# Attention and two feed-forward layers on one core: score limits built on GpSimd after the opening, and four numbers of the planner changed

## The chip, the cores and the metric

One core of one Trainium2 chip runs the whole program. The metric is device time in microseconds (us), the median of three runs. The program is one launch: weights, queries, keys and values come from HBM, and the result goes back there.

## What is computed

Attention on 4 batches, 8 heads, 576 positions, head size 64, with two kinds of mask, followed by two gated feed-forward layers (2304 tokens, 512 -> 2048 -> 512):

```python
scores = scale * np.matmul(q, k.transpose(0, 1, 3, 2))
mask_local = (rel >= 0) & (rel < stride)                       # heads 0-3, stride 32
mask_strided = (rel >= 0) & (pos[None, :] % stride == pos[:, None] % stride)  # heads 4-7
scores = np.where(masks[None, :, :, :], scores, -1000000000.0)
attn = softmax(scores)                                          # written out in the reference
x = np.matmul(attn, v)                                          # -> (2304, 512)
h = x @ w_in;  g = h * (1.0 / (1.0 + np.exp(-1.702 * h)));  x = g @ w_out      # first layer
h = x @ w_in;  g = h * (1.0 / (1.0 + np.exp(-h)));          out = g @ w_out    # second layer
```

## The kernel before

The tokens are cut into eight chunks of 288 (half a sequence each). For every chunk there is an attention (four pairs of heads, one local and one strided head in each) and a first layer of 16 blocks `f` into the hidden size and 16 out of it. Attention of chunk c runs between the matrix products of chunk c-1's first layer. Chunk 0 works in float32 (L858 and L888); the later chunks work in pairs of float16 numbers, high and low part (L861 and L892). The second layer (L1173, L1284) follows when the last first layer is done, and works with factors of sums and differences of weight blocks.

A pair of heads goes through these steps: score products on TensorE (L707), masking and maxima on VectorE, subtraction of the maximum on GpSimd or VectorE (L731), exponential on ScalarE (L733), sum and inverse on VectorE (L736 to L741), scaling on GpSimd (L743), three transposes on TensorE (L749), a copy out of PSUM (L753 or L754), and the product with the values (L784). Chunk 0 adds its mask by products with `rep` and `mk` (L679, L682). The later chunks take the minimum with a tile of limits `mt`: eight small operations (L595, L596) on 32 partitions build it, two products with `rep` (L603) spread it to 128 partitions, and VectorE copies it back (L609).

Weights of the first layer are converted from 64-bit to 32-bit numbers on the core. A block is loaded (L301), ScalarE takes out two parts (L454, L306), ScalarE or VectorE takes the sign (L313, L311), VectorE joins bits (L317), GpSimd adds (L322), and ScalarE or VectorE sums squares for a scale (L473, L475). The blocks of the input weights are numbered f0 to f15 here, those of the output weights likewise. The weights of the second layer are converted beside chunks 1 to 6, parked in HBM (L523), loaded again in pairs (L546, L547), turned into factors by adds (L536) and splits into high and low parts (L412, L560), and stored (L563).

The order of the work on each engine is made when the program is built, by the class `Planner`: a list scheduler in which every task has engines with costs, a priority (a due time), the earliest time `at` from which it may be taken, and a `margin` between the end of what it needs and the moment when it is offered to its engine. A DMA's result is taken to be there 2 us plus `late` after the link has carried it. These numbers only decide the order: on the chip each engine runs its list in order, and waits on semaphores for what it needs. The numbers that the change touches are `ACT_AT`, the `at` of ScalarE's first step on each block of the input weights; `MARGIN[0]`, the margin ahead of the transposes of chunks 1 to 7; `MASK`, the priority of the limits; and the loads of factors, which have no `late`.

Of the kernel before, what the change touches and what calls it, by code (L numbers as in the profile page):

```python
# [37 lines left out]
WIN0, WINS = 18.0, 1.95  # L38
WOUT0, WOUTS = 49.0, 1.95
SCALE = (52.0, 84.0)  # L40
ACT_AT = 13.0
LATE = 5.0
WSI = T1 - 24.0
WSO = T1 + 4.0
# [1 line left out]
FACT = (270.0, 21.0)  # L46
ATT0 = {"load": (0.0, 5.5), "s": 5.0, "step": 1.5, "av": (20.6, 21.0)}
VSP, AHEAD, PLOW = 7.0, 8.0, 30.0
MARGIN = (0.4, 1.5, 0.6)
GORDER = (((0, 1), (0, 1, 2)), ((0, 1), (3,)), ((2, 3), (0, 1, 2, 3)))  # L50
SIGN, NSD, V2, MASK = 0.6, 4, 15.0, 30.0
NORM = (20.0, 24.0)
# [156 lines left out]
def attention_moe_moe2_kernel(  # L209
# [16 lines left out]
    nc = tc.nc  # L226
# [18 lines left out]
    w2s = nc.dram_tensor("w2_scratch", (2, KF, 128, 512), F32, kind="Internal").ap()  # L245
# [84 lines left out]
    at = actx.enter_context(tc.tile_pool(name="at", bufs=1))  # L330
# [56 lines left out]
    for i in range(4):  # L387
# [3 lines left out]
    P = Planner({"ps": range(8), "rq": [0], "rk": [0], "rv0": [0], "rv1": [0],  # L391
                 "ek": range(2), "eq": [1], "-": [], "pair": [1], "x1": [0], "sl": range(NSM), "pt": range(NPT), "t": range(NTS),
                 "cv": range(NCV), "f": range(NF)} | {f"g{f}": [0] for f in range(KF)}, 0.30)
# [121 lines left out]
    k_parked = {}  # L515
# [23 lines left out]
    fed = [None]  # L539

    def factors(i, prio, k_s):

        a, b, u, v = (P.buf("f") for _ in range(4))
        A, B, U, V = (lambda x=x: wm[:, x.idx] for x in (a, b, u, v))
        load, prio = prio, prio + PLOW
        ka = P.dma(load - 8, 0.25, lambda on: nc.sync.dma_start(out=A(), in_=w2s[0, i]), [k_s, k_parked[0, i], fed[0]], [a, b], at=load - 12)  # L546
        kb = P.dma(load - 8, 0.25, lambda on: nc.sync.dma_start(out=B(), in_=w2s[0, i + 8]), [ka, k_parked[0, i + 8]], (), [b])  # L547
        lo = lambda X: lambda: X()[:, 0:256]
        hi = lambda X: lambda: X()[:, 256:512]
        k1 = any_add(prio, lo(U), lo(B), hi(B), ALU.add, [kb], [u, v], [b])  # L550
        k3 = any_add(prio, lo(V), lo(A), lo(B), ALU.subtract, [ka, kb, k1], (), [v, a, b])
        k2 = any_add(prio, hi(U), lo(U), lo(A), ALU.subtract, [k1, ka], (), [u, a])
        k4 = any_add(prio, hi(V), hi(A), hi(U), ALU.subtract, [k2, k3], (), [v, a, u])
        parts = ((a, A, 0, 2, [ka]), (b, hi(B), 2, 1, [kb]), (u, U, 3, 2, [k1, k2]), (v, V, 5, 2, [k3, k4]))
        fed[0] = k1
        for x, src, m, w, deps in parts:
            o = P.buf("f")
            O = lambda o=o, w=w: wm[:, o.idx].bitcast(F16).rearrange("p (h e) -> p h e", h=2)[:, :, 0:256 * w]
            h = P.add(any_hi(256 * w), prio, lambda on, O=O, src=src: put(on, O()[:, 0], src(), sc["wi"][0]), [k_s, *deps], [o], [x])
            k = P.add(dve_t(256 * w), prio, lambda on, O=O, src=src: nc.vector.scalar_tensor_tensor(  # L560
                out=O()[:, 1], in0=src(), scalar=sc["wi"][0], in1=O()[:, 0], op0=ALU.mult, op1=ALU.subtract),
                [h], (), [x, o], two=True)
            P.dma(load + 2, 0.125 * w, lambda on, O=O, m=m, w=w: nc.sync.dma_start(  # L563
                out=wfs[i, :, :, m:m + w, :].rearrange("p h m e -> p h (m e)"), in_=O()), [k], (), [o])
# [24 lines left out]
    def mask_tile():  # L589

        def limits(on):
            e = nc.gpsimd if on == "POOL" else nc.vector
            for z, g, m in ((0, 0, 0), (0, 1, 1), (1, 0, 0), (1, 1, 2)):
                to = mt[0:32, z, :, g]
                e.tensor_scalar(out=to, in0=mk[0:32, m], scalar1=-1.0, scalar2=BIG, op0=ALU.is_ge, op1=ALU.mult)  # L595
                e.tensor_tensor(out=to, in0=to, in1=mk[0:32, m], op=ALU.add)  # L596
        kl = P.add({"POOL": 4.0, "DVE": 2.6}, MASK, limits)
        ks, kc = [], []
        for z in range(2):
            p = P.buf("ps")  # L600

            def mm(on, z=z, p=p):
                nc.tensor.matmul(banks[p.idx][:, 0:2 * W * NLB], lhsT=rep[0:32], rhs=mt[0:32, z].rearrange("p b g w -> p (b g w)"),  # L603
                                 start=True, stop=True)
            ks.append(P.add({"PE": 0.25}, MASK + 2.0, mm, [kl], [p]))
            kc.append((z, p))
        for z, p in kc:
            def copy(on, z=z, p=p):
                nc.vector.tensor_copy(out=mt[:, z].rearrange("p b g w -> p (b g w)"), in_=banks[p.idx][:, 0:2 * W * NLB])  # L609
                if z == 0:  # L610
                    nc.vector.memset(mt[0:32, 0, 0, 0, 0:32], NEG)
            k_mask.append(P.add({"DVE": 0.7}, MASK + 4.0, copy, ks, (), [p]))

    def attention(c, b):
# [46 lines left out]
        if c == 1:  # L661
            mask_tile()
# [255 lines left out]
    for i in range(KF // 2):  # L918
# [34 lines left out]
          for i in range(2)]  # L953
# [7 lines left out]
    P = Planner({"t": range(NS - 10), "f": range(NS - 10, NS - 6), "x": range(NS - 6, NS - 2), "xv": range(NS - 2, NS), "y": [], "w": [],  # L961
                 "ps": range(8), "r": range(NS + 2, NS + 6), "v": [NS, NS + 1, NS + 6, NS + 7]}, 0.29)
# [442 lines left out]
```

## Time and profile before

| | us |
|---|---|
| median of 3 runs (820.1 to 823.79) | 820.96 |
| profiled execution, device time | 820.78 |
| its span, first to last instruction | 819.0 |
| TensorE busy | 797.8 |
| VectorE busy | 607.0 |
| ScalarE busy | 500.7 |
| GpSimd busy | 376.3 |

The profiled execution takes 1.78 us more than its span, and 0.18 us less than the median. TensorE (PE in the rows) is busy in 97% of the span, so the 21.2 us in which it stands idle are what a change of order can gain, and new idle time is what it can lose. A row of a timeline reads: start, duration, engine, line, operation, what is written and read, and in square brackets how long the engine stood idle before it and what ended that.

### The profile page before, as it was taken

Reading aid. Unit: us, or ns where it says so; the run is one execution under the profiler, and the core shown is the slowest. Engines: PE = TensorE matmul, PEld = TensorE weight load, DVE = VectorE, ACT = ScalarE, POOL = GpSimd, SP = SyncE. Lnnn points to the kernel's source line nnn. Section 1 sums busy time; section 2 is a strip of 40 time slices with the busy share of each in tenths; the row PEclk is TensorE's granted clock in tenths of the full one; section 3 lists DMA queues with packets and bytes.
Section 4 is the critical chain, followed back from the end, with each engine's and each line's share of the span. In section 5 each row is a group of like instructions: output and inputs, shape, how many; then the busy total and the mean of one; then the engine's idle time right before and its main releaser. Section 6 shows DMA issues by size and latency. Waiting matters only on the chain.

```text
span 819.0 us, 22334 instructions
## 1 busy us (share of the span) xinstructions
PE 797.8 (97%) x8910; PEld 666.7 (81%) x8910; DVE 607.0 (74%) x1177; ACT 500.7 (61%) x930; POOL 376.3 (46%) x403
## 2 busy tenths in 40 slices
PE   5999999999999989999999999999999999999998
PEld 3776767878878768778787788888889988888887
DVE  8999889268479587697663727789987799878652
ACT  3898867398587685777843334645544766645510
POOL 4667654024126166275332525788977553221200
PEclk9999999999999999999999999999999999999999
DMA  9989600763827867545315725666767898656501
GB/s 271 407 216 277 146 22 10 190 195 107 233 100 225 270 220 243 178 149 173 123 61 199 279 81 168 227 223 212 221 211 259 287 318 274 231 192 224 177 28 52
DMA packets 91221, 157.26 MB, mean 192 GB/s; under 512 B 9380, under 2 KB 49644, under 8 KB 91116
## 3 DMA queue, kind: packets, MB, share of 16 engines
q1 hardware_dynamic: 90556, 154.45, 58.9%
q8 instruction: 70, 1.15, 0.6%
q10 hardware_dynamic: 560, 1.38, 0.6%
q14 instruction: 35, 0.29, 0.1%
HBM read 102.31 MB, written 53.48 MB: 190 GB/s over the span
## 4 chain that ended last, share of the span: by engine, by line
PE 74%; DVE 10%; DMA 6%; ACT 3%; POOL 3%; issue 2%; SPq 1%; DVEq 0%; POOLq 0%; ACTq 0%
PE aps L1173 10%; PE aps L1284 9%; PE aps L892 6%; PE aps L861 6%; PE hps L1173 5%; PE gps L1173 5%; PE hps L1284 4%; PE hps L892 4%; PE gps L1284 4%; PE gps L861 3%; PE hps L861 3%; PE aps L858 2%; PE gps L892 2%; DMA rv<-in_v_dram 2%; DMA rk<-in_k_dram 2%
## 5 line engine op out<-in xcount | busy, mean ns | idle before, releaser
L1173 PEld LDWEIGHTS <-wf 128*128 128x128 f16 x1680 | 150.6, 98 | 15.4
L1284 PEld LDWEIGHTS <-wf 128*128 128x128 f16 x1512 | 147.6, 98 | 17.5 <-DVE wf L996 0.4
L861 PEld LDWEIGHTS <-regA 128*128 128x128 f16 x1152 | 111.3, 98 | 29.6 <-issue 1.1
L892 PEld LDWEIGHTS <-regB 128*128 128x128 f16 x1152 | 111.7, 98 | 27.3
L989 POOL TENSOR_TENSOR tt<-tt 128x256 f32<-128x256 f32 (+2 forms) x87 | 83.2, 966 | 59.5 <-DVE wf L996 32.9
L322 POOL TENSOR_TENSOR wm<-wm 128x512 int32<-128x512 int32 x32 | 46.1, 1444 | 79.2 <-DVE wm L317 65.0
L861 PE MATMUL aps<-x,regA 128*128 128x288 f16 x612 | 81.2, 286 | 0.1
L984 ACT ACTIVATE wf<-tt,xsg 128x512 f16<-128x512 f32 x88 | 58.9, 712 | 27.9 <-DMA tt<-g_scratch 9.1
L996 DVE SCALAR_TENSOR_TENSOR wf<-tt,xsg,wf 128x512 f16<-128x512 f32 x88 | 72.4, 857 | 1.1 <-ACT wf L984 1.1
L892 PE MATMUL aps<-g,regB 128*128 128x288 f16 x480 | 62.6, 286 | 0.0
L1284 PE MATMUL aps<-regA,wf 128*128 128x256 f16 x480 | 58.1, 273 | 0.1
L1173 PE MATMUL aps<-xfa,wf 128*128 128x256 f16 (+1 forms) x528 | 53.1, 256 | 0.0
L892 PE MATMUL hps<-g,regB 128*128 128x288 f16 x384 | 50.8, 286 | 0.0
L743 POOL TENSOR_TENSOR prt<-prt,sus 128x384 f32<-128x384 f32 x32 | 31.5, 987 | 31.3 <-DVE sus L741 29.2
L1185 ACT ACTIVATE tt<-tt 128x512 f32<-128x512 f32 x39 | 24.4, 626 | 29.7 <-DVE tt L1180 29.5
L731 POOL TENSOR_TENSOR prt<-prt,nms 128x384 f32<-128x384 f32 x21 | 18.9, 898 | 49.6 <-DVE nms L729 43.3
L861 PE MATMUL gps<-x,regA 128*128 128x288 f16 x300 | 40.6, 286 | 0.7 <-DVE g L417 0.7
L417 DVE SCALAR_TENSOR_TENSOR g<-aps,sg,g 128x288 f16<-128x288 f32 x51 | 25.8, 512 | 19.6 <-ACT g L410 19.3
L1173 PE MATMUL aps<-g,wf 128*128 128x256 f16 x324 | 38.8, 273 | 0.0
L1284 PE MATMUL aps<-regB,wf 128*128 128x256 f16 x312 | 38.0, 273 | 0.0
L892 PE MATMUL gps<-g,regB 128*128 128x288 f16 x288 | 37.6, 286 | 0.0
L869 ACT ACTIVATE aps<-aps,invh 128x288 f32<-128x288 f32 x51 | 24.1, 478 | 16.4 <-PE aps L861 15.7
(317 smaller groups left out, 1813.7 us busy)
## 6 DMA issues: line engine op xcount, KB each, us to landing
tt<-g_scratch SPq DMA_DIRECT2D x76, 256.0 KB
g_scratch<-tt SPq DMA_DIRECT2D x64, 256.0 KB
w<-in_moe_w_out_dram SPq DMA_DIRECT2D x25, 512.0 KB
regB<-in_moe_w_in_dram SPq DMA_DIRECT2D x16, 512.0 KB
w<-in_moe_w_in_dram SPq DMA_DIRECT2D x16, 512.0 KB
w_scratch<-wm SPq DMA_DIRECT2D x32, 256.0 KB
regB<-g_scratch SPq DMA_DIRECT2D x32, 256.0 KB
wf<-in_factors SPq DMA_DIRECT2D x8, 896.0 KB
```

The lines of the kernel that those rows point to most:

```text
L322: nc.gpsimd.tensor_tensor(out=di, in0=m.bitcast(I32), in1=di, op=ALU.add)
L417: dve_t(n), prio, lambda on: nc.vector.scalar_tensor_tensor(out=lo(), in0=src(), scalar=s(), in1=hi(), op0=ALU.mult, op1=ALU.subtract),
L743: kno = P.add({"POOL": 1.0}, t + 8, lambda on: nc.gpsimd.tensor_tensor(out=sets(N), in0=sets(N), in1=wide(sus[:, sl.idx], 2 * NLB), op=ALU ...
L861: nc.tensor.matmul(o, lhsT=pvA[:, f, x, kk, :], rhs=x1[:, y, kk, :], start=(i == 0), stop=(i == 3 * KD - 1))
L869: a = P.add(act_t(HS), t + 2, lambda on, p=p: nc.scalar.activation(out=banks[p.idx][:, 0:HS], in_=banks[p.idx][:, 0:HS], func=AF.Gelu_appr ...
L892: nc.tensor.matmul(o, lhsT=pvB[:, f, u, dt * 128:(dt + 1) * 128], rhs=g1[:, w, f, :], start=(f == 0 and j == 0), stop=(f == KF - 1 and j = ...
L984: nc.scalar.activation(out=out, in_=in_, func=AF.Copy, scale=s)
L989: return P.add({e: x for e, x in any_add(n).items() if e in by}, prio, lambda on: (nc.gpsimd if on == "POOL" else nc.vector).tensor_tensor ...
L996: dve_t(n), prio, lambda on: nc.vector.scalar_tensor_tensor(out=lo(), in0=src(), scalar=s(), in1=hi(), op0=ALU.mult, op1=ALU.subtract),
L1173: nc.tensor.matmul(place(b, f), lhsT=wf[:, nf * g + f, x, wa, 128 * kk:128 * kk + 128], rhs=rhs.rearrange("p (h t) -> p h t", h=2) if n2 = ...
L1185: return P.add(act_t(512), t + 5, lambda on: nc.scalar.activation(out=sl(b), in_=sl(b), func=AF.Silu), after, (), [b], tab="silu")
L1284: nc.tensor.matmul(bank(b)[:, 256 * half:256 * half + 256], lhsT=fb[:, x, a, 128 * f:128 * f + 128], rhs=wt[:, 4 * p + f, z, wi, :], start ...
```

## The change

Five edits. The limits may only be built on GpSimd (before: GpSimd or VectorE), and not before the planner's time 30, and the two products that spread them not before 34. ScalarE's first step on the input weights may be taken from 17 on (before: 13). The margin ahead of the transposes of chunks 1 to 7 is 1.2 (before: 0.4). A load for factors is taken to be there 2 us later.

```diff
-ACT_AT = 13.0
+ACT_AT = 17.0
-MARGIN = (0.4, 1.5, 0.6)
+MARGIN = (1.2, 1.5, 0.6)
+FLATE = 2.0
-        ka = P.dma(load - 8, 0.25, lambda on: nc.sync.dma_start(out=A(), in_=w2s[0, i]), [k_s, k_parked[0, i], fed[0]], [a, b], at=load - 12)
-        kb = P.dma(load - 8, 0.25, lambda on: nc.sync.dma_start(out=B(), in_=w2s[0, i + 8]), [ka, k_parked[0, i + 8]], (), [b])
+        ka = P.dma(load - 8, 0.25, lambda on: nc.sync.dma_start(out=A(), in_=w2s[0, i]), [k_s, k_parked[0, i], fed[0]], [a, b], at=load - 12, late=FLATE)
+        kb = P.dma(load - 8, 0.25, lambda on: nc.sync.dma_start(out=B(), in_=w2s[0, i + 8]), [ka, k_parked[0, i + 8]], (), [b], late=FLATE)
-            e = nc.gpsimd if on == "POOL" else nc.vector
+            e = nc.gpsimd
-        kl = P.add({"POOL": 4.0, "DVE": 2.6}, MASK, limits)
+        kl = P.add({"POOL": 4.0}, MASK, limits, at=MASK)
-            ks.append(P.add({"PE": 0.25}, MASK + 2.0, mm, [kl], [p]))
+            ks.append(P.add({"PE": 0.25}, MASK + 2.0, mm, [kl], [p], at=MASK + 4.0))
```

What the change does to the lists of the engines stands at three places. Lines after the change are one higher than before (L604 is L603 of before).

TensorE's first rows, before the change: `mt` are the limits, `rep` spreads them, `mk` is the mask of chunk 0.

```order
L603 LDWEIGHTS rep
L603 MATMUL hps<-mt,rep 128x384
L603 LDWEIGHTS rep
L603 MATMUL hps<-mt,rep 128x384
L679 LDWEIGHTS rep
L679 MATMUL gps<-mk,rep 128x192
```

The same place after the change, and then the place to which the two products have gone, among chunk 0's products with the input weights (`x_75` is the attention's result):

```order
L680 LDWEIGHTS rep
L680 MATMUL hps<-mk,rep 128x192
...
L859 MATMUL aps<-x_75,regA 128x288 x16
L604 LDWEIGHTS rep
L604 MATMUL hps<-mt,rep 128x384
...
L859 MATMUL gps<-x_75,regA 128x288 x4
```

Chunk 0's scores now stand first on TensorE, and the spreading stands after six blocks of chunk 0's first layer. VectorE loses the eight operations that stood ahead of its first maxima; its two copies of `mt` move behind eleven of the bit joins (L317).

GpSimd's rows behind the setup of the masks, before: `prt` are attention's probabilities (scaled by L743), `regA` the converted input weights.

```order
L743 TENSOR_TENSOR prt<-prt,sus 128x384 x2
L322 TENSOR_TENSOR regA<-wm,regA 128x512
L743 TENSOR_TENSOR prt<-prt,sus 128x384 x2
L322 TENSOR_TENSOR regA<-wm,regA 128x512 x15
L322 TENSOR_TENSOR regB<-wm,regB 128x512 x7
```

The same place after:

```order
L744 TENSOR_TENSOR prt<-prt,sus 128x384 x4
L323 TENSOR_TENSOR regA<-wm,regA 128x512 x7
L596 TENSOR_SCALAR mt<-mk 32x3x64
L597 TENSOR_TENSOR mt<-mt,mk 32x3x64
...
L323 TENSOR_TENSOR regA<-wm,regA 128x512 x9
L323 TENSOR_TENSOR regB<-wm,regB 128x512 x6
```

All four pairs of chunk 0 are scaled ahead of the first weight block, and the eight operations of the limits stand between the blocks f6 and f7. On ScalarE the first weight block moves from behind the second exponential to behind the fourth exponential and the second copy of transposed probabilities.

GpSimd at the attention of chunk 5, where the first factors are made, before: `wm` holds factors, with `s` their scale; L536 is an add of a factor, L412 the high part of a split, L731 and L743 belong to pairs of heads.

```order
L731 TENSOR_TENSOR prt<-prt,nms 128x384
L322 TENSOR_TENSOR wm<-wm 128x512
L412 TENSOR_SCALAR wm<-wm,s 128x256
L536 TENSOR_TENSOR wm<-wm 128x256
L731 TENSOR_TENSOR prt<-prt,nms 128x384
L743 TENSOR_TENSOR prt<-prt,sus 128x384
L536 TENSOR_TENSOR wm<-wm 128x256
L412 TENSOR_SCALAR wm<-wm,s 128x512 x3
L743 TENSOR_TENSOR prt<-prt,sus 128x384
```

The same place after:

```order
L732 TENSOR_TENSOR prt<-prt,nms 128x384
L323 TENSOR_TENSOR wm<-wm 128x512
L744 TENSOR_TENSOR prt<-prt,sus 128x384
L732 TENSOR_TENSOR prt<-prt,nms 128x384
L413 TENSOR_SCALAR wm<-wm,s 128x256
L537 TENSOR_TENSOR wm<-wm 128x256 x3
L413 TENSOR_SCALAR wm<-wm,s 128x512
L744 TENSOR_TENSOR prt<-prt,sus 128x384
L413 TENSOR_SCALAR wm<-wm,s 128x512 x2
```

Ahead of chunk 5's second scaling there stood three splits in a row; now there stand three adds and one split, and the other splits follow it. On SyncE the second load of the first factors (L547 before, L548 after) stood behind a store of a parked block (L523) and now stands ahead of it. On TensorE, of the 24 transposes of chunks 2 to 7, 21 keep the same products between them and their scores; two have one block of products more (third pair of chunk 2, second of chunk 3) and one has one block less (second of chunk 6). In chunk 1 three of the four stand two to five products of L888 later against their scores. The list of the second layer is the same on all engines.

## Rows read from the trace of the kernel before

**Rows 1.** Busy time by stretch: length, engines, granted clock (PEclk), DMA share, GB/s.
```profile
0.00:20.00 20.00, 10.03 (x255) 6.94 (x256) 16.37 (x48) 7.71 (x15) 8.66 (x26) 1.00 0.90 267
...
60.00:107.00 47.00, 44.34 (x533) 32.46 (x533) 41.92 (x82) 35.47 (x72) 32.52 (x29) 1.00 0.75 188
107.00:140.00 33.00, 31.32 (x420) 24.71 (x420) 30.18 (x73) 25.75 (x52) 13.83 (x18) 1.00 0.06 19
...
290.00:310.00 20.00, 17.45 (x280) 13.67 (x278) 17.37 (x43) 16.99 (x30) 13.26 (x17) 1.00 0.67 215
```

**Rows 2.** Waits of TensorE: line, releaser, us in total, times, longest.
```profile
PE hps L603 <- DVE mt L596: 7.8, 2, 7.4
PE gps L749 <- POOL prt L743: 2.5, 4, 1.0
PE aps L431 <- DVE wtout L437: 1.1, 1, 1.1
```

**Rows 3.** Timeline of the opening, VectorE's row first, then TensorE's.
```profile
6.25 0.18 DVE L371 COPY rep<-idb 32x128 bf16<-32x128 bf16 x1
```
```profile
8.25 0.47 PE L603 MATMUL hps<-mt,rep 32*128 32x384 bf16 x1 [0.41 <-DVE mt L596]
8.66 0.50 PE L679 MATMUL gps<-mk,rep 128*128 128x192 bf16 x2
...
16.64 0.90 PE L749 MATMUL aps<-idt,prt 128*128 128x128 f32 x3 [0.85 <-POOL prt L743]
...
18.23 2.86 PE L784 MATMUL aps<-ptt,rv 64*64 64x32 f32 x82 [0.34 <-ACT ptt L753]
...
25.91 4.21 PE L858 MATMUL aps<-x,regA 128*128 128x288 f32 x8
```

**Rows 4.** SyncE's DMA queue from 0 to 16 us: packets, MB, share.
```profile
q1 hardware_dynamic: 891, 2.44, 55.3%
```

**Rows 5.** Timelines of ScalarE and GpSimd: a copy of probabilities; weight blocks f5 to f7 and f15.
```profile
17.70 0.47 ACT L753 ACTIVATE ptt<-aps 128x384 f32<-128x384 f32 x1
```
```profile
29.00 4.17 POOL L322 TENSOR_TENSOR regA<-wm,regA 128x512 int32<-128x512 int32 x3 [0.58 <-DVE wm L317]
...
51.16 1.28 POOL L322 TENSOR_TENSOR regA<-wm,regA 128x512 int32<-128x512 int32 x1 [1.30 <-DVE wm L317]
```

**Rows 6.** GpSimd's groups nearest to the limits: busy, mean ns, idle before.
```profile
L366 POOL TENSOR_SCALAR_AFFINE_SELECT mk<-mk 32x192 bf16<-32x192 bf16 x2 | 0.7, 346 | 0.0
```
```profile
L536 POOL TENSOR_TENSOR wm<-wm 128x256 f32<-128x256 f32 x22 | 18.1, 833 | 5.3 <-DVE wm L536 3.6 <-ACT ts L835 0.7 <-DMA wm<-w_scratch 0.5
```

**Rows 7.** VectorE's squares of L475 from 20 to 60 us: ns, least/median/most.
```profile
L475 DVE SCALAR_TENSOR_TENSOR jv<-regA x12: 680/1298/1741, 23.7 to 57.3; 128x512 uint8<-128x512 f32 x12
```

**Rows 8.** Timelines at the weights' scales; last, TensorE's later product with values.
```profile
59.93 0.28 PE L431 MATMUL aps<-wtin,ones 128*128 128x1 f32 x2
...
106.38 0.38 PE L431 MATMUL aps<-wtout,ones 128*128 128x1 f32 x2 [1.07 <-DVE wtout L437]
```
```profile
59.61 0.17 DVE L437 TENSOR_REDUCE wtin<-acc 128x1 f32<-128x16 f32 x1
```
```profile
102.75 1.27 POOL L322 TENSOR_TENSOR regB<-wm,regB 128x512 int32<-128x512 int32 x1
```
```profile
89.24 1.48 PE L784 MATMUL aps<-ptt,rv 64*64 64x32 f32 x80
```

**Rows 9.** Chunk 5's second pair: VectorE, GpSimd, TensorE, and SyncE's load of factors.
```profile
299.90 0.19 DVE L741 RECIPROCAL sus<-sus 128x6 f32<-128x6 f32 x1
```
```profile
300.11 0.97 POOL L412 TENSOR_SCALAR wm<-wm,s 128x512 f16<-128x512 f32 x1 [0.92 <-DMA wm<-w_scratch]
301.06 1.25 POOL L743 TENSOR_TENSOR prt<-prt,sus 128x384 f32<-128x384 f32 x1
```
```profile
302.36 0.55 PE L749 MATMUL hps<-idt,prt 128*128 128x128 f32 x3 [2.17 <-POOL prt L743]
```
```profile
288.11 0.39 SPq L547 DMA_DIRECT2D wm<-w_scratch  x1
```

## The prediction

> **What bounds the kernel now.** I read the busy time by stretch first [rows 1]. TensorE is idle 9.97 us in the first 20 us, 2.66 us from 60 to 107, 1.68 us from 107 to 140 and 2.55 us from 290 to 310: 16.9 of its 21.2 idle us. Everywhere else it runs without a gap, and the change takes no product away and adds none. So the time can only move through these stretches, and through new idle time. Then the waits of TensorE [rows 2]: 7.8 us are its first two products, which spread the limits and wait for VectorE to build them; next come transposes that wait for GpSimd's scaling, and the scale of the output weights (L431), which waits for VectorE's sum. Last the timelines around these waits [rows 3, 8, 9].
>
> From 20 to 107 us the other engines are nearly as full as TensorE: from 60 to 107 VectorE works 41.9 of 47 us [rows 1]. A microsecond that TensorE gains in the opening is kept only where conversion, squares and splits of the weights come earlier too.
>
> **The opening.** Before, chunk 0's first product (L679, 8.66) stands behind the two products with the limits [rows 3]. Its own needs are older: the copy into `rep` ends at 6.25 + 0.18 = 6.43, and the queries and keys of the first heads were issued at once. With the limits gone from VectorE and the spreading gone from the front of TensorE, it can start at about 6.5: 2.16 us earlier. Maxima, exponentials and scaling follow it in a chain that has no weight work in it now. The second transposes, 16.64 before, end at 16.64 + 0.90 - 2.16 = 15.38; ScalarE copies at once, because the weight step that stood between is behind it now (0.47 us, rows 5): 15.85. Before, the product with the values ran from 18.23 [rows 3]. Its other need is the values: behind queries, keys and two weight blocks SyncE's queue has to bring 608 + 1024 + 576 KB = 2.26 MB by the shapes of the transfers, and it had moved 2.44 MB by 16.0 us [rows 4]. That lets the product start between 15.9 and 16.3; I take 16.1, a shift of 2.1 us. Then 2.86 us of product, two sets of transposes (2 x 0.90), a copy (0.5): second product at 21.2, chunk 0's layer at about 23.9 instead of 25.91. Shift: **2.0 us**.
>
> What is late next? Weights f0 and f1. ScalarE starts them at 15.85 and needs four steps of about 0.6 us, VectorE a join, GpSimd 1.27 to 1.4 us for each [rows 5]: both are there by 20.9, 3 us ahead of 23.9, so this delay by `ACT_AT` costs nothing. Its cover is the attention; without it, the same weight steps would hold TensorE by up to what they are late.
>
> The limits now take GpSimd's time between f6 and f7. No row has this operation on GpSimd. From below, eight times 0.35 us (a select on the same 32 x 192 tile) is 2.8 us; from above, eight times 0.83 us (an add on 128 x 256) is 6.7 us [rows 6]. I take 3.3, near the first, whose tile it is. Block f7 was done at 33.17 [rows 5] and would be done at about 36.5, at worst 39.9. Sixteen blocks take (59.93 - 25.91) / 16 = 2.13 us each [rows 3, 8], so TensorE wants f7 at 23.9 + 7 x 2.13 = 38.8. Covered at the value that I take; at the upper bound TensorE loses 1.1 us. The last block, done at 52.4, is wanted at 55.8, and GpSimd waited for VectorE before each block there, so the delay shrinks on the way.
>
> The two spreading products now stand in the full stretch. They took 0.47 us each at the opening's pace; the product with the values shows that pace to be half of the later one (82 products in 2.86 us against 80 in 1.48 [rows 3, 8], with the granted clock column at 1.00 in both stretches [rows 1]). So they cost 2 x 0.23 = 0.46 us. If the pace should rise at the same moment as before and not 2 us earlier, another 1.0 us is lost. Net shift at 60 us: 2.0 - 0.46 = **1.5 us**, between 0.5 and 2.2.
>
> **From 60 to 140 us.** Here the shift meets two gates. The scale of the input weights (L431) ran at 59.93, hardly after VectorE's sum at 59.61; the scale of the output weights at 106.38, after a wait of 1.07 us, for a chain that starts from the last output block on GpSimd at 102.75 [rows 8]. Where those stay, TensorE arrives 1.5 us earlier and waits 1.5 us longer. Three things move them earlier: attention frees VectorE and ScalarE about 2 us sooner, VectorE has the limits less ahead of everything (1.8 us, from 6.43 to 8.25 [rows 3]), and ScalarE waited for products of chunk 0 that come sooner now. Three hold them: VectorE has the two copies of the limits among the weight steps now, squares that it did early are put off, and GpSimd does more subtractions (24 instead of 21). I let two thirds pass: **-1.0 us**. Bounds: nothing passes (0), or all of it and half of the idle 4.3 us of these two stretches with it (-3.7).
>
> **Transposes and factors.** The margin bites less than its name: 21 of 24 transposes of chunks 2 to 7 keep their distance from the scores, and the pair of the 2.17 us wait [rows 9] is one of them. What changes for it is GpSimd's list. Its inverse was ready at 300.09, but GpSimd was in a split (300.11 to 301.06), after 0.92 us of waiting for a load of factors, and the scaling took until 302.31. Now adds and one split stand ahead of this scaling, and the load of the second half, issued at 288.11 behind a store [rows 9], comes earlier in SyncE's list. Without the split the scaling would end at 300.09 + 0.1 + 0.85 = 301.0, so the wait shrinks from 2.17 to about 0.85: **-1.3 us**. Bounds: the whole 2.55 us of that stretch, or as much again lost at another pair whose scaling is now behind adds. The loads' `late` costs nothing by itself: the factors are read by the second layer alone, whose first products stand behind the whole last first layer.
>
> **The sum.** 820.78 - 1.0 - 1.3 = 818.5 for an execution like the profiled one; the median of before is 0.18 higher, so 818.7.
>
> **The rivals.** (a) *The parts add up.* The gates move with the opening and the waits of the first layers shrink: -3.7, and the 2.55 us of 290 to 310 go: 820.96 - 6.2 = 814.8. For it: VectorE's list is shorter by nine squares over the first part (they went to ScalarE, which had 11.5 us idle from 60 to 107). Against: the lists of TensorE around both gates are unchanged. Chance 0.32.
>
> (b) *The gates eat it.* VectorE gets back as interference what it gave away: squares of 512 columns took 680 ns alone and up to 1741 ns beside GpSimd's adds [rows 7], and now 3.3 us more GpSimd work lies in that stretch. Three or four squares slowed by about 0.6 us each are 2 us of VectorE, and both sums at the gates come no earlier. Then 1.5 us at the opening become 1.5 us more of waiting, the waits at 302 reappear at a neighbouring pair, and the time is 820.96. Chance 0.20. The Trainium skill's page "SBUF — State Buffer" (section "SBUF: two separate sides") states such a rule against this change: the port pair that VectorE and GpSimd share is held by one instruction for its whole length, and a VectorE operation with two inputs in SBUF waits until GpSimd's is done. The spread from 680 to 1741 ns agrees with it; by it alone this rival would be the forecast.
>
> (c) *Slower.* GpSimd's list becomes the gate of attention in chunks 5 to 7. Scaling now stands behind up to four adds of factors, which wait for loads; if in each of these three chunks one pair more waits as the second pair of chunk 5 did, 3 x 2.17 = 6.5 us are added, and the opening's gain is lost at the gates: 827.5. It decides from the point at which a load lands after GpSimd has reached its add and a scaling is ready behind it. For it: GpSimd waited for loads of factors already, 0.92 us ahead of this split [rows 9]. Against: the larger `late` places users later. Chance 0.10.
>
> **How the numbers follow.** Forecast 818.7 with chance 0.38; (a) 0.32, (b) 0.20, (c) 0.10. A measurement of this kernel tells 0.5%, 4.1 us, from no change, so faster means below 816.9 and slower above 825.1. Faster: (a), less its upper edge, plus the forecast's lower edge: 0.35. Slower: (c) nearly whole: 0.09. The same: 0.56. Range: below, (a) with the other half of the first layers' waits gone too (814.8 - 2.1 = 812.7); above, (b) with one new wait of 2.2 us, 823.2; what is beyond is (c) and little of (a).
>
> **What would show it.** Right: TensorE's first product at about 6.5 us, the product with values near 16.1, chunk 0's layer near 23.9, no wait at L859 for weights; L431's second wait longer than 1.07 us but at an earlier moment than 106.38; the wait near 300 below 1 us. Wrong: a first product still near 8.7 us (queries not landed), a wait of L859 for f7 behind the limits, transposes of chunks 6 and 7 that wait for scaling, or a part from 310 us to the end that is no longer without gaps.

## The result, and the profile after

The changed kernel takes 827.06 us (median, 824.75 to 828.3) against 821.67 us of the kernel before in the same series: ratio 1.0057, 95% interval 1.0044 to 1.0069, so 4.7 us slower (the two medians lie 5.4 us apart). The forecast, 818.7 against 820.96, was 2.3 us faster. The profiled execution took 825.79 us, its span is 824.0. Lines are one higher than before (L432 is L431 of before).

Busy time by stretch after the change, columns as in [rows 1]; the stretch from 20 to 60 us stands here too:

```profile
0.00:20.00 20.00, 8.78 (x237) 6.21 (x238) 14.86 (x38) 6.66 (x12) 9.45 (x27) 1.00 0.90 239
20.00:60.00 40.00, 37.88 (x256) 29.33 (x253) 33.62 (x57) 32.82 (x67) 28.06 (x25) 1.00 0.97 331
60.00:107.00 47.00, 41.73 (x464) 31.14 (x463) 44.23 (x87) 33.80 (x68) 32.44 (x29) 0.93 0.70 190
107.00:140.00 33.00, 31.73 (x359) 24.71 (x358) 29.00 (x69) 25.09 (x54) 18.75 (x21) 1.00 0.06 19
290.00:310.00 20.00, 18.23 (x279) 14.24 (x262) 18.81 (x42) 19.85 (x35) 10.53 (x12) 1.00 0.49 172
```

Against [rows 1] TensorE is idle 1.25 us more in the opening (11.22 against 9.97) and 2.6 us more from 60 to 107 (5.27 against 2.66), and there its mean granted clock is 0.93 instead of 1.00. From 20 to 60 it is now idle 2.1 us, where it was 0.2 before:

```profile
20.00:60.00 40.00, 39.77 (x248) 31.29 (x244) 37.27 (x66) 35.08 (x75) 26.26 (x20) 1.00 0.95 319
```

From 107 to 140 and from 290 to 310 it is idle less, by 0.4 and 0.8 us. So the loss is made in the first 107 us, and the part that the margin was to bring is there, if smaller. The scale of the output weights (L432 on `wtout`) runs at 113.89 instead of 106.38, 7.5 us later, and the span is 5.0 us longer: 2.5 us come back behind it.

The waits of TensorE, as in [rows 2]:

```profile
PE hps L680 <- DVE rep L372: 6.5, 1, 6.5
PE gps L432 <- DVE wtin L438: 4.6, 1, 4.6
PE gps L785 <- ACT wm L455: 1.7, 1, 1.7
PE hps L859 <- DVE mt L612: 1.6, 1, 1.6
PE gps L785 <- DMA rv<-in_v_dram: 1.1, 2, 0.7
```

The 7.8 us for the limits [rows 2] are 6.5 us for `rep` now, as planned. In exchange there are waits at the product with the values (L785), for the limits' copies in the middle of chunk 0's layer, and one of 4.6 us for the scale of the input weights, which [rows 8] did not have.

The opening on TensorE, as in [rows 3], and SyncE's queue up to 16 us, as in [rows 4]:

```profile
6.49 0.50 PE L680 MATMUL hps<-mk,rep 128*128 128x192 bf16 x2 [6.49 <-DVE rep L372]
...
17.12 0.43 PE L785 MATMUL gps<-ptt,rv 64*64 64x32 f32 x8 [1.74 <-ACT wm L455]
18.23 0.43 PE L785 MATMUL gps<-ptt,rv 64*64 64x32 f32 x8 [0.68 <-DMA rv<-in_v_dram]
19.10 2.34 PE L785 MATMUL gps<-ptt,rv 64*64 64x32 f32 x68 [0.45 <-DMA rv<-in_v_dram]
...
26.25 3.92 PE L859 MATMUL hps<-x,regA 128*128 128x288 f32 x8
```
```profile
q1 hardware_dynamic: 814, 2.22, 50.8%
```

The first product starts at 6.49, 2.17 us earlier than in [rows 3]. The product with the values comes in three pieces as the values land, and most of it runs from 19.10. Chunk 0's layer starts at 26.25 against 25.91: nothing of the 2.17 us is left. Five kernels below (the margin, the slack, both, and the two with a wait put in) have the lists of before on every engine up to there, and start this layer between 25.90 and 27.27, so the 0.3 us between the two profiles say nothing.

The queue had moved 2.22 MB by 16 us, less than the 2.44 MB of [rows 4]. It moves as little without the change. The same row for the kernel before with the slack alone, and with slack and margin:

```profile
q1 hardware_dynamic: 808, 2.20, 52.4%
q1 hardware_dynamic: 784, 2.13, 50.4%
```

In the trace of before the last packet of the values' loads on this queue (3072 bytes each, a size that no other load there has) ends at 16.0 us, after the change at 18.2, and in the five kernels with the lists of before between 17.2 and 18.5. The one profile that the forecast could read was the earliest of them.

The limits on GpSimd, then VectorE behind them:

```profile
33.19 1.18 POOL L596 TENSOR_SCALAR mt<-mk 32x192 bf16<-32x192 bf16 x1
34.45 0.54 POOL L597 TENSOR_TENSOR mt<-mt,mk 32x192 bf16<-32x192 bf16 x1
...
39.75 0.54 POOL L597 TENSOR_TENSOR mt<-mt,mk 32x192 bf16<-32x192 bf16 x1
40.25 4.94 POOL L323 TENSOR_TENSOR regA<-wm,regA 128x512 int32<-128x512 int32 x4
```
```profile
41.55 4.20 DVE L476 SCALAR_TENSOR_TENSOR jv<-regA 128x512 uint8<-128x512 f32 x1 [2.92 <-POOL regA L323]
...
67.49 0.16 DVE L438 TENSOR_REDUCE wtin<-acc 128x1 f32<-128x16 f32 x1
```

The eight operations hold GpSimd from 33.19 to 40.29, 7.1 us. VectorE works on until 38.6 and then comes to its square of f7. It waits 2.92 us for f7's add, and then takes 4.20 us, where the shortest square of [rows 7] took 0.68. These are 2.9 + 3.5 = 6.4 us of an engine with little room, and its sum for the scale comes at 67.49, 7.9 us later than in [rows 8]. The copies of the limits, for which TensorE waits 1.6 us, stand behind the same square. TensorE at that place, and two stretches of it (clock: third number from the end):

```profile
67.70 0.58 PE L432 MATMUL gps<-wtin,ones 128*128 128x1 f32 x2 [4.61 <-DVE wtin L438]
...
69.02 2.29 PE L889 MATMUL aps<-g,regB 128*128 128x288 f32 x4
```
```profile
63.00:67.00 4.00, 0.10 (x1) 0.00 (x0) 3.91 (x7) 1.22 (x3) 2.92 (x2) 1.00 0.99 373
67.00:74.00 7.00, 6.30 (x90) 4.42 (x91) 6.78 (x20) 3.58 (x8) 4.05 (x5) 0.52 1.03 268
```

Behind 4.6 us without work TensorE runs at the lower of its two clock levels until about 74 us: four products take 2.29 us, which later in the same stage take 1.15. With 7 us at a granted 0.52, that is some 3 us more (an estimate from these rows).

### The profile page after: what moved, and what is told of

Its sections match the earlier page's. It is cut to its first block, busy times and chain, and to the rows that moved or that the text cites. A ratio compares the mean times of both kernels' runs of the same rounds, so it can differ in the third digit from the quotient of the medians.

```text
span 824.0 us, 22333 instructions
## 1 busy us (share of the span) xinstructions
PE 798.2 (97%) x8910; PEld 667.4 (81%) x8910; DVE 605.6 (73%) x1151; ACT 507.9 (62%) x948; POOL 381.0 (46%) x411
## 3 DMA queue, kind: packets, MB, share of 16 engines
q8 instruction: 70, 1.15, 0.6%
## 4 chain that ended last, share of the span: by engine, by line
PE 65%; DVE 8%; ACT 8%; DMA 5%; issue 3%; POOL 3%; SPq 1%; DVEq 0%; POOLq 0%; ACTq 0%
PE aps L1285 9%; PE aps L1174 9%; PE aps L893 5%; PE hps L1174 5%; PE aps L862 5%; PE hps L1285 4%; PE gps L1174 4%; PE gps L1285 3%; PE gps L893 3%; PE hps L893 2%; PE gps L862 2%; PE hps L862 2%; DMA in_factors<-wm 2%; DVE wf L997 2%; ACT g L411 2%
## 5 line engine op out<-in xcount | busy, mean ns | idle before, releaser
L862 PE MATMUL aps<-x,regA 128*128 128x288 f16 x624 | 83.1, 286 | 0.0
L893 PE MATMUL aps<-g,regB 128*128 128x288 f16 x624 | 81.3, 286 | 0.0
L323 POOL TENSOR_TENSOR wm<-wm 128x512 int32<-128x512 int32 x32 | 42.0, 1313 | 81.9 <-DVE wm L318 50.0
L732 POOL TENSOR_TENSOR prt<-prt,nms 128x384 f32<-128x384 f32 x24 | 22.9, 954 | 47.4 <-DVE nms L730 41.9
L893 PE MATMUL hps<-g,regB 128*128 128x288 f16 x288 | 38.1, 286 | 0.0
L862 PE MATMUL hps<-x,regA 128*128 128x288 f16 x276 | 37.1, 286 | 0.0
L862 PE MATMUL gps<-x,regA 128*128 128x288 f16 x252 | 34.0, 286 | 0.0
```

The costliest lines, as they stand in the source:

```text
L323: nc.gpsimd.tensor_tensor(out=di, in0=m.bitcast(I32), in1=di, op=ALU.add)
L862: nc.tensor.matmul(o, lhsT=pvA[:, f, x, kk, :], rhs=x1[:, y, kk, :], start=(i == 0), stop=(i == 3 * KD - 1))
L893: nc.tensor.matmul(o, lhsT=pvB[:, f, u, dt * 128:(dt + 1) * 128], rhs=g1[:, w, f, :], start=(f == 0 and j == 0), stop=(f == KF - 1 and j = ...
```

## The experiments

The expectations number the theories. 1: the limits between two of GpSimd's adds are the loss. 2: the later due time of the first weight steps is. 3: the loads of chunk 0's values bound the opening, so that it can't get shorter. 4: the edits let the planner find another order as a whole, and new waits come from that. Ratios are to the kernel before in the same series (821.7 to 823.6 us). The rows of a kernel come from one profiled execution, which need not be a typical one: the widest gap is 832.0 against a median of 826.4 us, for the changed kernel with the mask edit undone.

| kernel | ratio | 95% interval |
|---|---|---|
| mask edit alone | 1.0032 | 1.0019 to 1.0046 |
| due time 17 alone | 1.0031 | 1.0018 to 1.0043 |
| margin 1.2 alone | 0.9980 | 0.9968 to 0.9992 |
| slack of the factor loads alone | 0.9962 | 0.9945 to 0.9979 |
| changed, mask edit undone | 1.0046 | 1.0025 to 1.0068 |
| changed, due time undone | 1.0054 | 1.0038 to 1.0071 |
| changed, limits late on VectorE | 1.0032 | 1.0019 to 1.0046 |
| changed, limits early on GpSimd | 0.9988 | 0.9971 to 1.0004 |
| changed, same order, limits moved to the opening | 1.0024 | 1.0009 to 1.0039 |
| changed, same order, values loaded first | 1.0032 | 1.0019 to 1.0045 |
| changed, same order, both moved | 0.9979 | 0.9962 to 0.9996 |
| before, wait of 5.6 us put in | 1.0062 | 1.0044 to 1.0079 |
| before, wait of 2.7 us put in | 1.0037 | 1.0018 to 1.0056 |

**One edit alone, and one undone.** The mask edit on the kernel before, and the changed kernel without it:

```diff
-            e = nc.gpsimd if on == "POOL" else nc.vector
+            e = nc.gpsimd
...
-        kl = P.add({"POOL": 4.0, "DVE": 2.6}, MASK, limits)
+        kl = P.add({"POOL": 4.0}, MASK, limits, at=MASK)
...
-            ks.append(P.add({"PE": 0.25}, MASK + 2.0, mm, [kl], [p]))
+            ks.append(P.add({"PE": 0.25}, MASK + 2.0, mm, [kl], [p], at=MASK + 4.0))
```

> The kernel before with the mask edit as its only change: limits on GpSimd due at 30, spreading products due at 34. Theory 1: 825 to 828 us, with the eight operations taking about 7 us between two adds of GpSimd and VectorE's square behind them waiting 3 us. Theory 2: 818.5 to 821 us, as the earlier due time (13) keeps the conversions ahead of TensorE. Theory 3: chunk 0's AV products still start after 18 us although the first product runs at 6.5 us.

> The changed kernel with its mask edit alone taken back: the limits stand in the opening again, on VectorE, and the two spreading products ahead of chunk 0's scores; weight steps due at 17, the margins of the transposes and the slack of the factor loads stay as changed. Theory 1 (limits between the adds of GpSimd are the loss, about 1.9 us in 20 to 60 us and 2.6 us in 60 to 107 us): 820 to 821.5 us, no product of L889 or L859 waits for GpSimd or for the mask's copies before 107 us, and the wait of L432 for wtin falls from 4.6 us to about zero. Theory 2 (the later due time of the first weight steps is the loss): 825 to 827 us, with the 4.6 us wait still there. Theory 3 (the V loads bound the opening whatever the limits do): the first 20 us hold the same 8.8 us of products as with the edit.

Alone it costs 0.32%, with the same picture: the operations take 6.8 us between two adds, the wait for wtin is 3.7 us and the products with the values (AV products in the expectations) wait for the values; the scale of the output weights waits 2.6 us on top. But without it the other edits still cost 0.46%, which theory 1 did not allow. The first two rows are waits of the one, the last two of the other:

```profile
PE hps L431 <- DVE wtin L437: 3.7, 1, 3.7
PE aps L784 <- DMA rv<-in_v_dram: 2.2, 3, 0.9
```
```profile
109.88 0.59 PE L432 MATMUL aps<-wtout,ones 128*128 128x1 f32 x2 [2.58 <-DVE prt L726]
...
306.51 0.55 PE L750 MATMUL aps<-idt,prt 128*128 128x128 f32 x3 [2.84 <-POOL prt L744]
```

The second kernel has no wait for wtin and lost, in this execution, at two other places, each with a stretch of half clock behind it.

The due time alone (`ACT_AT` 17 instead of 13), and the changed kernel with 13:

> The kernel before with the first weight steps due at 17 instead of 13 as its only change. Theory 2 (this makes conversions late): 824 to 827 us with waits of TensorE for GpSimd's adds between 40 and 110 us. The prediction's step (no cost, 0.7 us of ScalarE freed at chunk 0's transposes): within 1 us of before. Theory 4: a wait of more than 2 us somewhere in 60 to 140 us, that before doesn't have.

> The changed kernel with the due time of the first weight steps back at 13 and all else as changed; the limits stand on GpSimd between the adds of f6 and f7 as in the changed kernel. If the 7.1 us there are the loss by themselves: 1.002 to 1.005 of before, with TensorE waiting 2.5 us or more at L432 for wtin. If the later due time together with the other order is the loss: 0.996 to 1.000.

Alone it costs 0.31%: in that order TensorE waits 2.6 us for the scale of the output weights, 1.07 in [rows 8], as its row of the waits shows:

```profile
PE aps L431 <- DVE wtout L437: 2.6, 1, 2.6
```

In the changed kernel taking it back gives nothing (1.0054 against 1.0057), and the wait for wtin is still 3.7 us. So theory 2 is not what made the changed kernel slower; the price of this edit depends on the order that it meets.

The margin alone (`MARGIN[0]` 1.2 instead of 0.4), and the slack of the factor loads alone (`late=FLATE`):

> The kernel before with the transposes' margin of 1.2 instead of 0.4 as its only change. The prediction's step: the waits of L749 for GpSimd (2.2 at 302 us, 2.5 in four shorter ones) halve, 821.5 to 823 us against 823.5. Theory 4: the attention's order moves as a whole, and a wait of over 2 us with a half clock behind it comes in somewhere in 60 to 310 us: 824 to 826 us.

> The kernel before with the slack of 2 for the loads of factors as its only change. The prediction's step (nothing to gain or lose, these loads had landed long before they are read): within 1 us of before, and no stretch ahead of 290 us differs. Theory 4 (any moved place can bring a wait): the waits between 290 and 440 us, 3.2 us in the kernel before, change by more than 1 us.

The margin gains 1.6 us; with it TensorE is idle 0.54 us from 290 to 310, instead of 2.55 [rows 1]:

```profile
290.00:310.00 20.00, 19.46 (x295) 15.13 (x293) 19.48 (x44) 16.06 (x28) 15.04 (x17) 1.00 0.57 189
```

The slack gains 3.1 us, more than either view said. TensorE's list is that of before up to the attention near 300 us, and in the profiled executions only 1.1 us of span is gained. A part of the other 2 us may be half clock that the profile of before does not have: of the 32 executions of before in this series, nine show a granted clock of 0.998 over the whole span and take 824.3 us on the mean, four show 1.00 and take 822.7; of the eight with the slack none shows 0.998, and five at 1.00 take 820.0. Between those at 1.00 there are still 2.7 us, and why stays open. Both together (limits and due time as before):

> The changed kernel with both losing edits taken back: limits on VectorE in the opening and first weight steps due at 13; margin 1.2 and the factor loads' slack stay. If the edits' single prices add up (margin alone was 0.998 of before): 0.997 to 0.999, with no half clock. If the order that the planner finds matters more than the edits: a wait of over 2.5 us with a half clock behind it, and 1.000 to 1.004.

Measured 0.9967 (0.9954 to 0.9981): faster than both kernels, but not the sum of the two.

**The limits, with and without a new order.** Here every engine's list is that of the changed kernel, but the eight operations stand on GpSimd behind its memsets of the opening:

```diff
     for i in range(4):
         nc.gpsimd.memset(rk[64:128, i // 2, i % 2, 0:KO], 0.0)
+    for z, g, m in ((0, 0, 0), (0, 1, 1), (1, 0, 0), (1, 1, 2)):
+        to = mt[0:32, z, :, g]
+        nc.gpsimd.tensor_scalar(out=to, in0=mk[0:32, m], scalar1=-1.0, scalar2=BIG, op0=ALU.is_ge, op1=ALU.mult)
+        nc.gpsimd.tensor_tensor(out=to, in0=to, in1=mk[0:32, m], op=ALU.add)
...
         def limits(on):
-            e = nc.gpsimd
...
+            return
```

> The changed kernel with every engine's order as it is, except that the eight operations of the limits stand on GpSimd right behind its memsets of the opening instead of between the adds of f6 and f7 (the planned step stays, but issues nothing). It takes the 7.1 us away from that place and nothing else. Theory 1 (the 7.1 us there are the loss, with TensorE's wait of 4.6 us for wtin and its half clock behind it): the wait for wtin falls below 1 us, no half clock at 67 us, and 818.5 to 821.5 us against 823.5 of before in this series. Theory 4 (the other order that the three other edits bring is the loss): 824 to 827 us, and the wait for wtin stays above 2 us or another wait of 107 to 310 us takes its place.

The ratio falls from 1.0057 to 1.0024, about 2.7 us. With the wait that is left this is what theory 4 said (824 to 827 against 823.5), and not theory 1. The operations now take 5.9 us where GpSimd was idle, and the sum for wtin comes at 63.58 instead of 67.49 (lines from L432 on four higher):

```profile
63.58 0.16 DVE L442 TENSOR_REDUCE wtin<-acc 128x1 f32<-128x16 f32 x1
```

TensorE still waits 2.8 us for it: in this order VectorE has four squares of input blocks between 53.6 and 62.0, where the list of before has two behind 50.5. Waits of TensorE:

```profile
PE gps L785 <- issue: 3.5, 1, 3.5
PE gps L436 <- DVE wtin L442: 2.8, 1, 2.8
PE gps L785 <- DMA rv<-in_v_dram: 2.0, 2, 1.3
```

The first of them is a stop inside a list of products with values, with no releaser. TensorE starts that list at 92.41, 4.2 us ahead of the changed kernel (96.58), and is at the scale of the output weights at 113.31, 0.6 us ahead (113.89): the stop and half clock behind it (94.7 to 101.6 us) take most of the gain back. In how many executions it stands is not known, so what this order costs without the limits stays open.

Two versions in which the planner was free to reorder: the limits due at 30 on VectorE (`P.add({"DVE": 2.6}, MASK, limits, at=MASK)`), and on GpSimd without a due time (`P.add({"POOL": 4.0}, MASK, limits)`):

> The changed kernel with the limits at the same late place but on VectorE (8 operations of 0.1 to 0.3 us in the opening of the kernel before). It parts where the limits stand from which engine computes them. Theory 1 (the 7.1 us on GpSimd are the loss): 819.5 to 822 us. Rival (late limits anywhere hold a PSUM bank and push the squares and sums): 824 to 827 us. If the opening gain exists at all it shows here as L859 starting before 25.9 us; theory 3 says 26 us or later.

> The changed kernel with the limits on GpSimd but without the due time, so that they stand ahead of chunk 0's multiplications, where GpSimd was idle from 5.4 to 11.8 us; the spreading products stay late. Theory 1: the 7.1 us would end at about 12.5 us, 0.7 us behind the first multiplication's operands, and nothing later is late: 819.5 to 822 us. Rival (GpSimd's work slows VectorE beside it, here the maxima and subtractions of chunk 0, by the factor that the square of 4.20 us showed): the softmax of chunk 0 is 2 us or more later, and the time is 823 to 826 us. Theory 2: 825 us or more.

On VectorE an operation takes 0.23 us instead of 1.18, and still the ratio is 1.0032, as the rival said: there is no wait for wtin, but one of 3.8 us at a score product (L708) that waits for VectorE's masking. Early on GpSimd they are done at 11.5 us, and the ratio is 0.9988, 0.7 us above theory 1's bounds, with the start of chunk 0's layer at 26.7. Both have another order, so neither prices the limits by themselves.

**What a wait of TensorE costs there.** The kernel before, its order kept, with unused squares on VectorE ahead of the sum for wtin, 8 as shown and 4 in the second kernel:

```diff
+        def total(on):
+            for i in range(8 if n == 0 else 0):
+                nc.vector.scalar_tensor_tensor(out=jv[:, 0:512], in0=regA[:, 1], scalar=1.0, in1=regA[:, 1], op0=ALU.mult, op1=ALU.mult)
+            nc.vector.tensor_reduce(out=tot1, in_=acc[:, n, :], axis=AX.X, op=ALU.add)
...
```

> The kernel before in its own order, with eight more squares of 128x512 on VectorE (0.68 us each, 5.4 us, results unused) ahead of the sum for wtin, so that TensorE's product of L431 at 59.9 us waits some 5 us. It prices one such wait by itself. If a wait costs its own length: +5.0 to +5.4 us. If TensorE's clock halves behind it, as at 67.7 to 74 us in the changed kernel: the granted clock shows 0.5 for some us behind the wait and the time grows by 7 to 9 us. If later slack gives it back: under +3 us.

> The kernel before in its own order with four more squares on VectorE ahead of the sum for wtin instead of eight (2.7 us instead of 5.4). The eight cost 1.0062 (5.1 us, 5.55 us of wait with half clock for 3.5 us behind it). If the price is in proportion: 1.003. If a short wait leaves the clock alone and later slack takes part of it: 1.000 to 1.002 with the granted clock at 1.00 throughout.

They cost 5.1 us (3.6 to 6.5) and 3.0 us (1.5 to 4.6). TensorE with the long wait, then with the short one:

```profile
65.53 0.58 PE L431 MATMUL aps<-wtin,ones 128*128 128x1 f32 x2 [5.55 <-DVE wtin L440]
65.97 1.31 PE L891 MATMUL aps<-g,regB 128*128 128x288 f32 x2
67.07 1.17 PE L891 MATMUL gps<-g,regB 128*128 128x288 f32 x2
```
```profile
61.75 0.38 PE L431 MATMUL aps<-wtin,ones 128*128 128x1 f32 x2 [2.66 <-DVE wtin L440]
61.99 0.73 PE L891 MATMUL aps<-g,regB 128*128 128x288 f32 x2
62.56 0.65 PE L891 MATMUL gps<-g,regB 128*128 128x288 f32 x2
```

A microsecond of wait at this gate costs about a microsecond. Behind 5.55 us the products run at half pace until 69 us (pairs of 1.17 us instead of 0.65), behind 2.66 us at full pace. In the profile of the long wait TensorE is 7.4 us later than before where the half clock ends, and 5.7 us later from 74 to 290 us: two waits of before at score products, 0.69 us at 64.91 and 0.50 at 68.38, are gone, and with them nearly all that the half clock cost (1.8 us). Nothing behind gives back the rest. Near 308 us, behind the 2.17 us wait of [rows 9], this execution runs at half clock again, and the profile of before does not; some two microseconds behind that wait, before and with the long wait put in:

```profile
304.00:305.00 1.00, 1.00 (x11) 0.80 (x9) 0.96 (x5) 1.00 (x2) 0.00 (x0) 1.00 0.88 125
309.00:310.00 1.00, 1.00 (x6) 0.62 (x5) 0.97 (x5) 1.00 (x3) 0.00 (x0) 0.50 0.53 117
```

**The values' loads.** SyncE's three loads of chunk 0's values ahead of the first two weight blocks. In the changed kernel this moves nothing else on any engine:

```diff
-ATT0 = {"load": (0.0, 5.5), "s": 5.0, "step": 1.5, "av": (20.6, 21.0)}
+ATT0 = {"load": (0.0, 2.0), "s": 5.0, "step": 1.5, "av": (20.6, 21.0)}
```

> The changed kernel with the three V loads of SyncE ahead of the first two weight blocks, nothing else. Theory 3: the waits for V at 17.1 to 19.1 us go, L859 starts 1.5 to 2 us earlier than at 26.25 us. As long as the 7.1 us of limits bind, that is not seen in the total: 1.003 to 1.006, since TensorE then waits longer for wtin. If the order behind it moves so that the limits hurt less: 1.000 or below.

TensorE's opening, and its wait for wtin:

```profile
15.96 2.86 PE L785 MATMUL gps<-ptt,rv 64*64 64x32 f32 x82 [0.23 <-ACT ptt L754]
...
23.62 4.21 PE L859 MATMUL hps<-x,regA 128*128 128x288 f32 x8
```
```profile
65.04 0.59 PE L432 MATMUL gps<-wtin,ones 128*128 128x1 f32 x2 [4.59 <-DMA w<-in_moe_w_out_dram]
```
```profile
64.83 0.16 DVE L438 TENSOR_REDUCE wtin<-acc 128x1 f32<-128x16 f32 x1
```

All waits for the values are gone, also the 1.74 us that the profile had put down to a weight step of ScalarE. Chunk 0's layer starts at 23.62, 2.6 us earlier than in the changed kernel and earlier than in any kernel with the old place. TensorE's product at the gate runs 2.7 us earlier behind a wait of the same length (the profile puts it down to a load, but VectorE's sum ended at 64.99), and the sum itself comes 2.7 us earlier: here the shift passes the gate whole. The ratio falls to 1.0032. So the opening's gain is real, and the place of these loads had eaten it. With the limits moved as well:

> The changed kernel's order on every engine with two things moved and nothing else: SyncE's three V loads of chunk 0 ahead of the first two weight blocks, and the limits' eight operations on GpSimd in the opening. Each alone gave back part of the 0.57% (V loads: 1.0032; limits: 1.0024). If the two are the whole loss and add up: 0.999 to 1.001 of before, with L859 starting at 23.5 to 25 us and no wait over 2 us for wtin. If they hide behind one another, or the rest of the order is a loss by itself: 1.002 to 1.004.

Measured 0.9979, 1.7 us faster than before and below the expectation's 0.999 to 1.001, although a wait for wtin is left (L436, 2.4 us; the expectation had none over 2). Chunk 0's layer starts at 23.93. By the ratios this is 6.4 us less than the changed kernel takes; the two parts alone gave 2.0 and 2.7, each with an interval of more than 1 us to either side. Waits that are left:

```profile
PE gps L436 <- DMA rv<-in_v_dram: 2.4, 1, 2.4
PE gps L785 <- issue: 2.2, 1, 2.2
```

The stop inside a list of products with values is here too. With every list kept, moving these two turns a loss of 0.57% into a gain of 0.21%, so they account for the loss of the changed kernel. In other orders the loads' place does not bring the same:

> As the run before, but with the limits on GpSimd ahead of chunk 0's multiplications (without a due time, 5.4 to 11.5 us, where GpSimd is idle) and the spreading products due at 34. It asks for the opening's gain without the 7.1 us between the adds. If the opening is bound by the limits: L859 starts at 24 to 25 us and the ratio is 0.995 to 0.998. Theory 3 (the V loads bound it): L859 starts at 25.5 to 26.7 us, TensorE waits 1 to 3 us at its AV products for V, and the ratio is 0.998 to 1.001.

> As the run before, with the three V loads of SyncE ahead of the first two weight blocks in its queue (due at 2.0 instead of 5.5). Theory 3: the AV products start at 15.5 to 16.5 us without a wait for V, L859 at 23.5 to 25 us, and the time is 1 to 2 us under the run before, unless f0 and f1 are now the ones that are late. Rival (the weights bound it as well): the waits for V go, L859 waits for f0's or f1's add of GpSimd instead, and the start of L859 stays at 25.5 us or later.

> Margin 1.2 and the factor loads' slack, limits on VectorE in the opening, due time 13 (0.9967 of before by itself), and the three V loads of SyncE ahead of the first two weight blocks. If the V loads' place is worth the same here as on GpSimd's version (0.9963 against 0.9995): 0.993 to 0.995. If the opening is bound by the limits' copies (7.8 us of wait, AV products at 17.5 us): 0.996 to 0.998.

The three gave 0.9995 (0.9982 to 1.0008), 0.9963 (0.9950 to 0.9977) and 0.9996 (0.9979 to 1.0013). In the second, the waits for values are gone and others for copies by ScalarE stand there, and chunk 0's layer starts at 27.0, not earlier than in the first (26.8). So the start that the rival gave held, though not by the adds of f0 and f1, and the gain lies behind the opening. The third did worse than either view said: its opening is bound by the limits' copies, and a stop of 3.6 us inside a list of products with values near 93 us is followed by half clock. The best kernels (0.9962, 0.9963, 0.9967) can't be told apart.

## Why the prediction was wrong, step by step

- **No gap elsewhere:** not so, by the prediction's own sum: 4.3 of the 21.2 idle us lie outside its four stretches, 3.5 of them behind 440 us. After the change it is 3.8 there, so nothing hangs on it.
- **First product at 6.5:** right (6.49). Its chain up to the second transposes ended at 14.47 + 0.90 = 15.37, forecast 15.38.
- **Values there by 15.9 to 16.3:** wrong, and the first failed step. It took what the queue had moved by 16.0 us in one execution [rows 4] for what it always brings. In that execution the values' last packet did end at 16.0. But the 2.44 MB left only 8% of room over the 2.26 MB needed, and with the same lists up to there it ended between 17.2 and 18.5 in five other profiles; after the change it was 18.2, and the last products with values could start at 19.10. With the loads placed first the product ran at 15.96 and the layer at 23.62, as forecast (16.1, 23.9). It cost about 2.0 us. Why the queue is faster in one execution than in another stays open.
- **The due time costs nothing:** right in the changed kernel (1.0054 without it), wrong as a statement on the edit (1.0031 alone).
- **The limits take 3.3 us of GpSimd:** wrong, the second failed step, worth about 2.7 us, which its interval does not part from the 2.0 of the first. They took 6.56 us of work, near the upper bound of [rows 6] (6.7), and 7.1 with the gaps. The row of that bound, an add on four times as many partitions, was the nearer one in time. The cover was also asked for at the wrong place: the prediction compared f7 with the moment when TensorE wants it, and TensorE did not wait for f7. VectorE did, with a square in its list, and what stands behind that square goes to the gate at L432.
- **Two thirds of the shift pass the gates, -1.0 us:** wrong as a result. The sum for wtin came 7.9 us later instead of 1 us earlier, and the wait there went from nothing to 4.61 us. That gate was the right place to look at [rows 8], and the prediction named what would hold VectorE's sum, but its worst bound was a sum that comes no earlier; one that comes later was not in it.
- **The wait at 302, -1.3 us:** right in kind. The margin alone gave 1.6 us, and from 290 to 310 the changed kernel is idle 0.8 us less. The slack of the factor loads "costs nothing by itself"; it gained 0.38% alone, and why is not settled.
- **The rivals:** (b) had the mechanism, GpSimd's added work in VectorE's way, but with squares slowed by 0.6 us and a loss that only ate the gain. One square of 4.20 us behind 2.92 us of wait was more than the three or four slowed ones together. The Trainium skill's page "SBUF — State Buffer" (section "SBUF: two separate sides") says that a VectorE operation with two inputs in SBUF waits until GpSimd's is done; that square ended at 45.75, within 0.6 us of GpSimd's four adds (45.19), which agrees in kind, though the square stood through three of these adds and not one. (c) gave nearly the measured time (827.5), but by a mechanism, GpSimd's list gating the transposes of chunks 5 to 7, that did not show: from 310 to 440 us TensorE is idle 0.05 us.

What stays open: the four edits alone add up to +0.05%, together they cost 0.57%, so the edits' effects depend on one another by half a per cent, and no single row carries that (the changed kernel without the mask edit, 1.0046, is the clearest case).

## What to carry to other kernels

Where work is moved to an idle-looking engine, follow what is queued behind it on the engine that waits for it, up to the next gate of the busiest engine; the first consumer in the product list may not be the one that waits. A load that one profile shows in time by a few tenths of a microsecond is not in time: here it came up to 2.5 us later in other executions with the same lists. An earlier chain in front of it needs the load moved too. Where a planner makes the order, price an edit by keeping the order and moving only its work: here edits measured alone did not add up, but the two parts moved in an unchanged order did, within their intervals.

## What the runs showed of the hardware

A comparison with multiply on 32 x 192 bf16 took GpSimd 1.18 us while VectorE worked, 0.85 us while it didn't or did small steps, and VectorE 0.23 us. Past the opening TensorE ran at half clock behind all stops from 2.8 to 5.55 us in these profiles, and behind some of the shorter ones: behind 1.96, 2.11, 2.44 and 2.58 us, but not behind 2.10 and 2.66. The 2.17 us wait of [rows 9] had it in one execution and not in another with the same lists around it, so the length of the wait alone does not say when. In three kernels' profiles TensorE stops for 2.2 to 3.6 us inside a list of products with values, after 17 of 80 in two of them, with no releaser that the profile shows; there was traffic on an instruction queue within some us, but so there was in stretches without a stop, and the cause stays open. One of them:

```profile
92.41 0.47 PE L785 MATMUL gps<-ptt,rv 64*64 64x32 f32 x17
96.34 2.13 PE L785 MATMUL gps<-ptt,rv 64*64 64x32 f32 x63 [3.46 <-issue]
```
